# Second MoE product of eight token blocks in seven half-size products instead of eight, with operand sums on GpSimd and new orders

## The chip, the cores and the metric

The kernel runs on one core of a Trainium2 chip. TensorE (PE; its weight loads are shown as PEld), VectorE (DVE), ScalarE (ACT) and GpSimd (POOL) compute, and SyncE (SP) issues nearly all DMAs. The metric is the time of one execution on the device in microseconds, as the median of several runs.

## The reference, cut to what matters

Attention over 8 batches, 8 heads and 1152 positions of 64 numbers, with queries averaged in pairs; its output, 4608 tokens of 512 numbers, goes through a small MoE: the larger of two products, and a second product of that.

```python
q_pool = q.reshape(B, H, S // 2, 2, D).mean(axis=3)
scores = q_pool @ k.transpose(0, 1, 3, 2) / sqrt(D)
attn = softmax(scores) @ v                                   # exp, divided by its row sum
x = attn.transpose(0, 2, 1, 3).reshape(4608, 512)
g = np.maximum(x @ w1, x @ w2)                               # 4608 x 1024
out = g @ w_out                                              # 4608 x 512
```

All inputs and the output are float32.

## The kernel before, in words

**Recording.** The kernel is written as a list of operations, each with the keys that it reads and writes (`Plan.op`). `reorder` then puts each engine's operations in an order that is written out by hand as a text, one letter or digit for each operation (`pe_order`, `dve_order`, `act_order`, `pool_order`, `sp_order`), and `solve` sets the semaphore waits. Every engine works through its own list in order. A digit in `pe_order` is the PSUM bank on which a job does its next piece; `jobs_of` lists which jobs follow each other on a bank. S is a score group.

**Attention.** Heads are handled in 32 pairs. For each pair K, Q and V are loaded in float32 (three buffers each) and cast to bf16 on POOL: `cast_k` (L457), `cast_q` (the sum of two neighbours, L490), `cast_v` (L496). K is transposed by a DMA on the SP queue (L476). Q is transposed on VectorE by `qtrans_dve` (L546) in eight pieces of 32 partitions and 9 x 32 elements, since a transpose there works inside blocks of 32 x 32. The scores are made in 324 groups of 512 columns for both heads (L678): two matmuls run side by side, one on each half of the array's rows (a *duo*). ScalarE takes the exponential of each group (L685), out of three PSUM tiles, from group 21 on out of two. The averages over V (a, L589 with 128 rows, L601 for the last half tile) take nine matmuls of 65 columns a piece; a pair has two jobs, of five and four pieces. VectorE divides (L611, L615, L619), and the result is transposed to `xT`, mostly by DMA (L725), in part on TensorE (L737).

**MoE.** The larger of two products is rewritten: with wd = w1 - w2, g = relu(x wd) + x w2, so that out = relu(x wd) w_out + x (w2 w_out). wd is made on POOL (L770) and w21 = w2 w_out on TensorE (L802). The first product is done in 13 token blocks (H while scores last, as duos, L877; h afterwards, with all rows, L850); its rectified tiles go to `gT`, a ring of 1024 tokens. The second product (P, L910) takes 256 tokens at a time: 12 steps of contraction (4 of x with w21, 8 of gT with w_out), each with two token tiles of 128 on two banks, and each once for each half of the rows: 24 duos of 512 columns. The halves are swapped between the two *turns*, and the first matmul of the second turn waits for the first turn to end (`fence`). VectorE copies both banks out at once (L919) and SP stores them. The last six tiles are done one by one with all rows (p, L940), after the last score group.

Of the kernel before, what the change touches and what calls it, by code (L numbers as in the profile page):

```python
# [9 lines left out]
P = 128  # L10
# [9 lines left out]
class Plan:  # L20
# [26 lines left out]
    def lane(self, o):  # L47
# [3 lines left out]
        if o["eng"] == "POOL":  # L51
            return {"kb": "k", "wd": "d"}.get(key[:2], key[0])
# [5 lines left out]
        return {"qt": "T", "w2": "W", "wo": "W", "gd": "G"}.get(key[:2], "Q")  # L58
# [234 lines left out]
def bass_funnel_attn__then__act_maxout2_kernel(  # L293
# [23 lines left out]
    RING = 1024  # L317
    assert D == 64 and S == NT * P and QU == NT and C == H * D and E == 512
# [13 lines left out]
    with outer:  # L332
# [23 lines left out]
        xT = sbuf([P, NC_, NTOK], BF16, "xT")  # L356
# [6 lines left out]
        w2b = xT[:, :, 512:1536]  # L363
        w2T = xT[:, :, 1536:2560].rearrange("p c (f x) -> p c f x", x=P)
        w2f = xT[:, :, 2560:4608].bitcast(FP32)
# [3 lines left out]
        osb = [osb2[:, s, :] for s in range(4)]  # L369

# [132 lines left out]
        def dve(fn, r, w):  # L503
            op("DVE", fn, r=r, w=w)
# [35 lines left out]
        def qtrans_dve(i, n):  # L540
            s, z = i % 2, i % 3
            h, pb, db = n // 4, n // 2 % 2, n % 2
            src, dst = 64 * h + 32 * pb, 64 * h + 32 * db
            view = qpT[z][:, :].rearrange("p (u x) -> p u x", x=HP)
            last = [f"qpT{z}"] + (["qpT0.0"] if i == 3 else []) if n == 7 else []
            op("DVE", lambda e: e.transpose(  # L546
                view[dst:dst + 32, :, 32 * pb:32 * pb + 32],
                qpf[s][src:src + 32, :, 32 * db:32 * db + 32]),
                r=[f"qp{s}.0", f"qp{s}.1"], w=[f"qt{z}.{n}"] + last, after=[f"qpT{z}"] + (["qpT0.0"] if i == 3 else []))
# [114 lines left out]
        def skeys(g):  # L664
            return [key for i, t, lo, *_ in pieces(g) for key in (
                f"kT{i % 3}.{t}", "qpT0.0" if i == 0 and lo < QA else f"qpT{i % 3}")] + [
                f"qt{i % 3}.{n}" for i in pairs_of(g) if i >= Q_PE for n in range(8)]
# [62 lines left out]
        def xtrans_pe(i):  # L730
# [9 lines left out]
            def evac(m):  # L740
                mb = fb[m][:, :].bitcast(BF16)
                op("DVE", lambda e: e.tensor_copy(xT[:, ct, b * SQ:b * SQ + SQ], mb[:, 0:SQ]),  # L742
# [4 lines left out]
        def xkeys(ct, n0, n1):  # L747
            return [f"xT.{ct}.{j}" for j in range(n0 // HP, n1 // HP)]
# [40 lines left out]
        ocount = [0]  # L789
# [24 lines left out]
        def store(lo, s, c0=0, c1=E, engs=("SP", "SP")):  # L814
# [436 lines left out]
```

## Time and profile before

| what | us |
|---|---|
| median of 3 runs (lowest, highest) | 362.35 (362.02, 362.59) |
| span of the profiled execution | 361.7 |
| first and last exponential begin | 6.4, 329.8 |
| last score matmuls begin | 329.2 |
| last matmuls end | 358.6 |
| K, Q, V loads, from issue to landing (median) | 6.4, 6.0, 6.3 |

The granted clock of TensorE is 0.999 over the span. Score groups run from about 6 to 330 us; all other matmuls stand between them in `pe_order`, and the last block's share of the MoE follows them. In the prediction a row of a timeline has the start, the duration, the engine, the line, the operation, the tiles (written<-read), the shape and the count of merged instructions; a row of a group has the total of busy time, the mean of one in ns, and the idle time before them with what ended it. A row of the waits has the waiting engine and line, whom it waited for, the total, and how many times.

### The profile page before, as it was taken

To read this page: it belongs to the slowest core of one execution; us is meant where nothing else is said; L and a number is where in the kernel's file an instruction comes from. 1 tells how busy PE (TensorE), PEld (TensorE's weight loads), DVE (VectorE), ACT (ScalarE), POOL (GpSimd) and SP (SyncE) were. 2 spreads that over 40 slices of the span, in tenths; PEclk is the share of its full clock that TensorE was granted. 3 is DMA by queue.
4 is the path that set the end of the run, shared out by engine and by line. 5 is a ranking of instruction groups with operands and counts; after the bars stand their busy time and mean duration, and the time that the engine had idled before them with its cause. 6 is when DMAs were issued, how large, how long until landed. Compare 5 with 4: busy or idle time off the path is not lost.

```text
span 361.7 us, 13398 instructions
## 1 busy us (share of the span) xinstructions
PE 355.0 (98%) x5973; PEld 222.1 (61%) x5973; DVE 243.1 (67%) x528; ACT 313.3 (87%) x355; POOL 124.5 (34%) x111
## 2 busy tenths in 40 slices
PE   8899999999999999999999999999999999999996
PEld 6666655566564666657575666666666565656753
DVE  3676787877589777866876687595977747625411
ACT  5999989989999999998999999989999988994221
POOL 1248967333055324452242426261234440010000
PEclk9999999999999999999999999999999999999999
DMA  7999999999959998997999999998999560805215
GB/s 239 408 394 398 402 286 296 244 286 344 246 123 242 284 302 235 251 256 179 285 309 184 269 277 284 305 251 202 243 215 269 169 153 15 198 16 87 52 30 147
DMA packets 77789, 84.76 MB, mean 234 GB/s; under 512 B 50080, under 2 KB 50848, under 8 KB 77728
## 3 DMA queue, kind: packets, MB, share of 16 engines
q1 hardware_dynamic: 77168, 83.09, 87.6%
q8 instruction: 47, 0.77, 0.9%
q10 hardware_dynamic: 560, 0.79, 0.6%
q14 instruction: 14, 0.11, 0.1%
HBM read 62.91 MB, written 9.44 MB: 200 GB/s over the span
## 4 chain that ended last, share of the span: by engine, by line
PE 93%; ACT 5%; issue 0%; DVE 0%; DVEq 0%
PE sps L678 20%; PE sps L589 13%; PE sps L910 12%; PE fb L910 10%; PE sps L877 9%; PE fb L589 7%; PE fb L877 7%; ACT et L685 5%; PE sps L940 3%; PE sps L601 2%; PE fb L802 2%; PE fb L940 1%; PE sps L850 1%; PE fb L601 1%; PE fb L850 1%; PE fb L411 1%
## 5 line engine op out<-in xcount | busy, mean ns | idle before, releaser
L685 ACT ACTIVATE et<-sps 128x1024 bf16<-128x1024 f32 (+1 forms) x336 | 305.2, 1009 | 20.5 <-PE sps L678 19.3
L678 PE MATMUL sps<-qpT,kT 64*128 64x256 bf16 (+7 forms) x1162 | 119.8, 284 | 1.7 <-DVE qpT L536 0.7
L546 DVE STREAM_TRANSPOSE qpT<-qp 32x288 bf16<-32x288 bf16 x216 | 101.4, 469 | 4.5
L678 PEld LDWEIGHTS sps<-qpT,kT 64*128 64x128 bf16 x1162 | 47.3, 94 | 51.1 <-ACT et L685 19.9
L490 POOL TENSOR_TENSOR qp<-qraw 128x576 bf16<-128x576 f32 x30 | 42.2, 1406 | 83.1 <-DVE qpT L546 58.6
L496 POOL TENSOR_SCALAR vE<-vraw 128x1152 bf16<-128x1152 f32 x32 | 36.8, 1152 | 62.8 <-DMA vraw<-in_v_dram 48.1
L589 PE MATMUL sps<-vE,et 128*128 128x65 bf16 x1440 | 51.2, 193 | 0.6 <-issue 0.4
L589 PEld LDWEIGHTS sps<-vE,et 128*128 128x128 bf16 x1440 | 46.0, 97 | 6.9 <-issue 5.4
L457 POOL TENSOR_SCALAR kbf<-kraw 128x1152 bf16<-128x1152 f32 x31 | 35.6, 1151 | 42.2 <-DMA kraw<-in_k_dram 29.6
L877 PE MATMUL sps<-xT,wd 64*128 64x512 bf16 (+3 forms) x368 | 42.8, 326 | 0.1
L910 PE MATMUL sps<-wo,stage 64*128 64x512 bf16 x256 | 37.5, 377 | 0.0
L877 PE MATMUL fb<-xT,wd 64*128 64x512 bf16 (+3 forms) x272 | 33.0, 334 | 0.1
L887 DVE TENSOR_SCALAR stage<-sps 128x1024 bf16<-128x1024 f32 (+3 forms) x23 | 22.3, 969 | 15.4 <-PE sps L877 15.2
L910 PE MATMUL fb<-wo,stage 64*128 64x512 bf16 x224 | 32.5, 377 | 0.0
L589 PE MATMUL fb<-vE,et 128*128 128x65 bf16 x864 | 30.5, 193 | 0.0
L589 PEld LDWEIGHTS fb<-vE,et 128*128 128x128 bf16 x864 | 27.5, 97 | 4.2 <-issue 3.2
L887 DVE TENSOR_SCALAR stage<-fb 128x1024 bf16<-128x1024 f32 (+3 forms) x17 | 17.0, 999 | 10.4 <-PE fb L877 10.1
L877 PEld LDWEIGHTS sps<-xT,wd 64*128 64x128 bf16 x368 | 15.6, 94 | 12.0 <-DVE xT L742 0.8
L611 DVE RECIPROCAL rcs<-sps 128x5 f32<-128x5 f32 (+1 forms) x40 | 7.3, 183 | 19.4 <-PE sps L589 18.7
L919 DVE COPY stage<-sps 128x1024 f32<-128x1024 f32 x8 | 9.8, 1224 | 13.8 <-PE sps L910 13.8
L910 PE MATMUL sps<-w,xT 64*128 64x512 bf16 x128 | 18.6, 377 | 0.0
L910 PE MATMUL fb<-w,xT 64*128 64x512 bf16 x112 | 18.1, 377 | 0.0
(94 smaller groups left out, 286.3 us busy)
## 6 DMA issues: line engine op xcount, KB each, us to landing
vraw<-in_v_dram SPq DMA_DIRECT2D x32, 576.0 KB, 6.3
kraw<-in_k_dram SPq DMA_DIRECT2D x31, 576.0 KB, 6.4
qraw<-in_q_dram SPq DMA_DIRECT2D x31, 576.0 KB, 6.0
out_dram<-stage SPq DMA_DIRECT2D x21, 256.0 KB, 5.4
out_dram<-stage SPq DMA_DIRECT2D x23, 128.0 KB, 3.0
xT<-in_moe_w_dram SPq DMA_DIRECT2D x4, 512.0 KB, 10.7
stage<-in_moe_w_out_dram SPq DMA_DIRECT2D x4, 512.0 KB, 13.7
stage<-in_moe_w_dram SPq DMA_DIRECT2D x4, 512.0 KB, 13.4
```

Source lines behind the costliest of these rows:

```text
L457: op("POOL", lambda g: g.tensor_scalar(kbf[s][:, :, :, :].rearrange("p t h d -> p h t d"), kraw[r][:, :, :, :], 1.0, 1.0, ALU.mult, ALU.mu ...
L490: op("POOL", lambda g: g.tensor_tensor(qpf[s][:, :, :], qraw[r][:, :, 0, :], qraw[r][:, :, 1, :], ALU.add), r=[f"qraw{r}"], w=[f"qp{s}.0", ...
L496: op("POOL", lambda g: g.tensor_scalar(vE[r][:, :, :, 0:D].rearrange("p t h d -> p h t d"), vraw[r][:, :, :, :], 1.0, 1.0, ALU.mult, ALU.m ...
L546: op("DVE", lambda e: e.transpose(view[dst:dst + 32, :, 32 * pb:32 * pb + 32], qpf[s][src:src + 32, :, 32 * db:32 * db + 32]), r=[f"qp{s}. ...
L589: last = e.matmul(fb[m][:, sb * 66:sb * 66 + 65], et[:, a:a + P], vE[vs][:, t, half, 0:65], start=(t == 0), stop=(t == NT - 1))
L601: last = e.matmul(fb[m][rows(half), NCH * 66:NCH * 66 + 65], et[:, a:a + NB], vE[vs][:, t, half, 0:65], start=(t == 0), stop=(t == NT - 1))
L678: last = e.matmul(sps[r][:, h, col:col + hi - lo], kT[i % 3][rows(h), t, :], qpT[i % 3][rows(h), lo:hi], start=True, stop=True)
L685: op("ACT", lambda e: e.activation(et2[:, :, c:c + z - a], sps[r][:, :, a - g * W:z - g * W], EXP, scale=scale), r=[f"s{r}"], w=keys + ([f ...
L877: last = e.matmul(fb[m + k][:, 0:size], wd[z, ct, (f0 + k) * P:(f0 + k + 1) * P], xT[z, ct, n0:n1], start=(turn == 0 and ct == 0), stop=(t ...
L887: dve(lambda e: e.tensor_scalar_max(gT[:, f0:f0 + 2, g0:g0 + size], wide[m // 2][:, :, 0:size], 0.0), [f"f{m}", f"f{m + 1}"], w + [f"f{m}" ...
L910: last = e.matmul(fb[m + k][:, :], lhs, rhs, start=(turn == 0 and j == 0), stop=(turn == 1 and j == NC_ + NF - 1))
L940: return e.matmul(fb[m][:, 0:c1 - c0], lhs, rhs[:, c0:c1], start=(j == 0), stop=(j == NC_ + NF - 1))
```

## The change

Tokens 512 to 4607 are now handled in eight blocks of 512 (`p_block`), by the Winograd form of Strassen's scheme. The four token tiles are split into rows 0 (tiles 0 and 2) and 1 (tiles 1 and 3), the contraction into two halves of six steps, the output into two halves of 256 columns. Seven products of a quarter of the size give the block; each has 6 steps x 2 token tiles x 2 row halves = 24 matmuls of 256 columns, 12 duos. Four jobs hold them (two, two, two and one products); tokens 0 to 511 are still done by `p_pair` (named P0.5 and P256.5), and the tiles that were done one by one at the end now belong to the last two blocks.

The operands that are sums are made on POOL: `t_sums` once for the weights (4 sums in two parts), `s_sums` for each block (4 sums in two parts, of 512 elements from `xT` and of 1024 from `gT`; where a ring's end cuts a block, in two pieces). VectorE adds the products up while it empties the banks (`end1` to `end4`).

To make room `xT` becomes a ring of 2304 tokens, and the float32 copy of w2 moves to a tile `extra`, where the sums live later. The query transposes become one of the full 128 x 576 tile and four that put the off-diagonal 32 x 32 corners right. All four engines' order texts, `sp_order` and the jobs' banks are new.

```diff
+    XRING = NTOK // 2
+    KT = (NC_ + NF) // 2
...
-        xT = sbuf([P, NC_, NTOK], BF16, "xT")
+        xT = sbuf([P, NC_, XRING], BF16, "xT")
+        extra = sbuf([P, NC_ * XRING], BF16, "extra")
...
         def qtrans_dve(i, n):
...
-            op("DVE", lambda e: e.transpose(
-                view[dst:dst + 32, :, 32 * pb:32 * pb + 32],
-                qpf[s][src:src + 32, :, 32 * db:32 * db + 32]),
+            if n == 0:
+                dst, src = qpT[z][:, :], qpf[s].rearrange("p u d -> p (u d)")
+            else:
+                h, pb = (n - 1) // 2, (n - 1) % 2
+                db = 1 - pb
+                to, at = 64 * h + 32 * db, 64 * h + 32 * pb
+                dst = view[to:to + 32, :, 32 * pb:32 * pb + 32]
+                src = qpf[s][at:at + 32, :, 32 * db:32 * db + 32]
+            op("DVE", lambda e: e.transpose(dst, src),
...
+        def t_sums(n, at):
...
+            op("POOL", lambda g: g.tensor_tensor(t(n), one, two, ALU.subtract),
+               r=r, w=[f"tw{n}.{at}"], after=[f"w2f{c}" for c in range(NC_)], fence=True)
...
+        def s_sums(lo, n, at):
+            t0, t1 = ((0, 2), (2, KT))[at]
+            a11, a12, a21, a22 = ((0, 0), (0, 1), (1, 0), (1, 1))
+            one, two, alu, dst = ((a21, a22, ALU.add, 0), (0, a11, ALU.subtract, 1),
+                                  (a11, a21, ALU.subtract, 2), (a12, 1, ALU.subtract, 1))[n]
...
+                op("POOL", lambda g, js=js, view=view: g.tensor_tensor(
+                    sx[dst][:, t0:t1, js, :], view(one, v1), view(two, v2), alu),
+                    r=r1 + r2, w=[f"sx{dst}.{at}"], after=[f"w2f{NC_ - 1}", f"wof{NC_ - 1}"], fence=True)
+
+        def p_block(lo):
...
+                def pair(e, m):
+                    for t in ts:
+                        for k in range(2):
+                            z = rows(turn ^ k)
+                            lhs, rhs = left(a, k, t)[0], right(b, t)[0]
+                            last = e.matmul(
+                                fb[m + k][:, x * HE:x * HE + HE], lhs[z, :], rhs[z, :],
+                                start=opening and t == 0, stop=closing and t == KT - 1)
+                    return last
...
+            def end1(m):
+                dve(lambda e: e.tensor_copy(part[:, :, 0, :], bank(m, X0)), [f"f{m}", f"f{m + 1}"], ["p1"])
+                add(m, part[:, :, 1, :], part[:, :, 0, :], bank(m, X1), ["p1"], ["u2"], True)
...
+            def end4(m):
+                if final:
+                    for j in range(2):
+                        add(m, osb[2 * j][:, HE:E], part[:, j, 1, :], bank(m, X0)[:, j, :], ["u2"], [f"osb{2 * j}"],
+                            j == 1)
+                        store(lo + 2 * j * P, 2 * j, HE, E, ("SP", "ACT"))
+                    return
...
+            return [Job(stage_units(ps), end) for ps, end in (
+                (((X0, A11, B11), (X1, 1, 1)), end1),
+                (((X0, A12, B21), (X1, 2, 2)), end2),
+                (((X0, 0, 0), (X1, A22, 3)), end3),
+                (((X0, 1, B22),), end4))]
...
-            "4": "p3840.0",
+            "4": "h10.3 h10.7 P3584.0 h11.0 h11.5 P4096.2",
...
-            "qvvqkkqvv")
+            "rsqksvqsskvrrqkvqkvssssrkqssvqskssrvqkvssqkvrsqkssqksrvvsvsrssssrssrssrsssrsssss")
```

Three places show what the new orders move. The first is TensorE between score groups 225 and 233, where the averages of pair 21 stand (L589 and L601, now L604 and L616; scores L678, now L693; second product L910, now L995). A row is the line, the operation, written<-read, the size that is written, and the count. Before:

```order
L910 MATMUL fb<-wo,stage 128x512 x6
L678 MATMUL sps<-qpT,kT 128x512 x2
L910 MATMUL fb<-wo,stage 128x512 x4
L678 MATMUL sps<-qpT,kT 128x64 x2
L678 MATMUL sps<-qpT,kT 128x448 x2
L601 MATMUL sps<-vE,et 64x65 x18
L589 MATMUL sps<-vE,et 128x65 x36
L678 MATMUL sps<-qpT,kT 128x128 x2
L678 MATMUL sps<-qpT,kT 128x384 x2
L678 MATMUL sps<-qpT,kT 128x192 x2
L678 MATMUL sps<-qpT,kT 128x320 x2
L589 MATMUL sps<-vE,et 128x65 x36
```

Now:

```order
L616 MATMUL sps<-vE,et 64x65 x18
L693 MATMUL sps<-qpT,kT 128x256 x4
L604 MATMUL sps<-vE,et 128x65 x36
L693 MATMUL sps<-qpT,kT 128x320 x2
L693 MATMUL sps<-qpT,kT 128x192 x2
L693 MATMUL sps<-qpT,kT 128x384 x2
L693 MATMUL sps<-qpT,kT 128x128 x2
L604 MATMUL sps<-vE,et 128x65 x36
L693 MATMUL sps<-qpT,kT 128x448 x2
L693 MATMUL sps<-qpT,kT 128x64 x2
L995 MATMUL fb<-w,xT 128x256 x4
L995 MATMUL fb<-wo,stage 128x256 x8
```

The two stretches of averages of pair 21 have become three, with score groups between.

The second place is the end of POOL's list. Before, the casts of the last pairs end it:

```order
L490 TENSOR_TENSOR qp<-qraw 128x576
L457 TENSOR_SCALAR kbf<-kraw 128x2x9x64 x2
L490 TENSOR_TENSOR qp<-qraw 128x576
L496 TENSOR_SCALAR vE<-vraw 128x2x9x64 x2
L1192 TENSOR_LOAD flag
```

Now sums of operands (L963; 512 elements from xT, 1024 from gT, which lies in `stage`) end it:

```order
L963 TENSOR_TENSOR stage<-xT 128x512
L963 TENSOR_TENSOR extra<-xT,extra 128x512
L963 TENSOR_TENSOR extra<-stage,extra 128x1024
L963 TENSOR_TENSOR extra<-xT 128x512
L963 TENSOR_TENSOR stage<-stage 128x1024
L963 TENSOR_TENSOR extra<-stage 128x1024
L963 TENSOR_TENSOR extra<-extra,xT 128x512
L963 TENSOR_TENSOR extra<-extra,stage 128x1024
L963 TENSOR_TENSOR extra<-xT,extra 128x512
L963 TENSOR_TENSOR extra<-stage,extra 128x1024
L1382 TENSOR_LOAD flag
```

Behind the last cast of V there are now 22 sums, for the last three blocks; the rows shown are S2 (small) of the last block, S3 of the block before, and then S0, S2, S1 and S3 of the last.

The third place is the end of TensorE's list. Before, the last tile's full-row matmuls end it:

```order
L940 MATMUL sps<-wo,stage 128x512 x6
L940 MATMUL sps<-wo,stage 128x384
L940 MATMUL sps<-wo,stage 128x512 x3
L940 MATMUL sps<-wo,stage 128x384 x7
L940 MATMUL sps<-w,xT 128x128 x4
L940 MATMUL sps<-wo,stage 128x128 x8
```

Now the last block's products do, those with a sum as left operand reading `extra`:

```order
L995 MATMUL sps<-w,xT 128x256 x4
L995 MATMUL sps<-wo,stage 128x256 x8
L995 MATMUL sps<-extra 128x256 x16
L995 MATMUL fb<-wo,stage 128x256 x8
L995 MATMUL fb<-extra,stage 128x256 x12
L995 MATMUL sps<-extra 128x256 x8
L995 MATMUL sps<-extra,xT 128x256 x4
L995 MATMUL sps<-extra,stage 128x256 x8
L995 MATMUL sps<-w,extra 128x256 x4
L995 MATMUL sps<-wo,extra 128x256 x8
L995 MATMUL sps<-w,extra 128x256 x4
L995 MATMUL sps<-wo,extra 128x256 x8
```

The last 24 matmuls are the product of S3, the sum that POOL makes last; ahead of them stand the products of S0, S1 and S2 of the same block.

More of the change, by code (lines that the diff above doesn't have):

```diff
@@ L501, in unit, with dve @@
             return lambda m: op("PE", lambda e: go(e, m), r=r, w=[f"f{m}"])
-        def dve(fn, r, w):
-            op("DVE", fn, r=r, w=w)
+        def dve(fn, r, w, after=()):
+            op("DVE", fn, r=r, w=w, after=after)
         def qtrans(i):
@@ L747, in xkeys @@
         def xkeys(ct, n0, n1):
-            return [f"xT.{ct}.{j}" for j in range(n0 // HP, n1 // HP)]
+            return [f"xT.{ct}.{j % (XRING // HP)}" for j in range(n0 // HP, n1 // HP)]
         def w_load(part, c):
@@ L878, in pair @@
                                 fb[m + k][:, 0:size], wd[z, ct, (f0 + k) * P:(f0 + k + 1) * P],
-                                xT[z, ct, n0:n1], start=(turn == 0 and ct == 0),
+                                xT[z, ct, n0 % XRING:n0 % XRING + size], start=(turn == 0 and ct == 0),
                                 stop=(turn == 1 and ct == NC_ - 1))
@@ new lines, in tiles, with akeys, ablocks @@
+        def tiles(lo, row):
+            return [lo + (2 * j + row) * P for j in range(2)]
+        def akeys(lo, row, k, at):
+            ns = tiles(lo, row)
+            if at == 0:
+                return [key for n in ns for c in range(2) for key in xkeys(2 * k + c, n, n + P)]
+            return [f"gT.{n % RING // P}.{4 * k + f}" for n in ns for f in range(4)]
+        def ablocks(lo, row, k, at):
+            src, w, size = ((xT, 2, XRING), (gT, 4, RING))[at]
+            full = src[:, k * w:k * w + w, :]
+            a = lo % size
+            if a + 4 * P <= size:
+                return [(slice(0, 2), full[:, :, a:a + 4 * P].rearrange("p t (j r x) -> p t j r x", r=2, x=P)[
+                    :, :, :, row, :])]
+            return [(slice(j, j + 1), full[:, :, n % size:n % size + P].unsqueeze(2))
+                    for j, n in enumerate(tiles(lo, row))]
@@ L1071, in chores, with fed @@
                 if i >= Q_PE:
-                    later(f"q{i}", [f"cq{i}"], lambda i=i: [qtrans_dve(i, n) for n in range(8)], free)
+                    later(f"q{i}", [f"cq{i}"], lambda i=i: [qtrans_dve(i, n) for n in range(5)], free)
                 if f"x{i}" not in on_pe:
                     later(f"x{i}", [f"a{i}"] + over(i), lambda i=i: xtrans(i))
+            ready = [f"wc{n}.{ct}" for n, ct in W_CASTS] + [f"wd{ct}.{half}" for ct, half in W_DIFFS]
+            for n in range(4):
+                for at in range(2):
+                    later(f"t{n}.{at}", ready + ["W0", "W2"][:2 - 2 * at] + [f"t{m}.{at}" for m in range(n)],
+                          lambda n=n, at=at: t_sums(n, at))
+            units = sorted({int(name[1:-2]) for v in jobs_of.values() for name in v.split()
+                            if name[0] == "P" and name.endswith(".0")})
+            for lo, back in zip(units, [None] + units):
+                def fed(row, k, lo=lo):
+                    return [f"H{nb}.{f}" if f"H{nb}" in count else f"h{nb}.{f + g}"
+                            for nb, (n0, n1) in enumerate(hblocks)
+                            if any(n0 < n + P and n < n1 for n in tiles(lo, row))
+                            for f in range(4 * k, 4 * k + 4, 2) for g in ((0,) if f"H{nb}" in count else (0, 1))]
+                here = [f"x{i}" for i in range(lo // SQ * NHP, ((lo + 4 * P - 1) // SQ + 1) * NHP)]
+                for n, dst in enumerate((0, 1, 2, 1)):
+                    for at in range(2):
+                        own = (fed(1, 0) + fed(1, 1), fed(0, 0), fed(0, 0) + fed(1, 0), fed(0, 1))[n]
+                        need = ready + (own if at else here) + [f"s{lo}.{m}.{at}" for m in ((), (0,), (), (1,))[n]]
+                        if n == 3:
+                            need.append(f"P{lo}.0")
+                        elif back is not None:
+                            need.append(f"P{back}.{(2, 3, 1)[n]}")
+                        later(f"s{lo}.{n}.{at}", need, lambda lo=lo, n=n, at=at: s_sums(lo, n, at))
         def more_banks(groups):
@@ L1194, in bass_funnel_attn__then__act_maxout2_kernel @@
         engs = (("POOL", nc.gpsimd), ("SP", nc.sync), ("DVE", nc.vector), ("ACT", nc.scalar), ("PE", nc.tensor))
-        first = {"POOL": 33, "SP": 66, "DVE": 92, "ACT": 61, "PE": 208}
+        first = {"POOL": 33, "SP": 66, "DVE": 88, "ACT": 61, "PE": 208}
         early = {"SP": 7, "ACT": 12, "DVE": 3}
```

207 lines of the change are left out of this document (144 added, 63 removed), and 31 rows, old and new, of the table jobs_of.

## The prediction

> **What bounds the kernel now.** I read first the busy shares and the chain of work that ended last, on the page, then the busy time of each engine in two stretches: from the end of score group 72 to the end of the last exponential (75.8 to 330.8 us), and from there to the end.
>
> ```profile
> PE 355.0 (98%) x5973; PEld 222.1 (61%) x5973; DVE 243.1 (67%) x528; ACT 313.3 (87%) x355; POOL 124.5 (34%) x111
> PE 93%; ACT 5%; issue 0%; DVE 0%; DVEq 0%
> 75.80:330.80 255.00, 254.86 (x4415) 156.76 (x4412) 179.33 (x388) 238.15 (x261) 84.20 (x69) 1.00 0.92 226
> 330.80:361.70 30.90, 27.80 (x277) 18.23 (x275) 10.32 (x28) 6.04 (x17) 0.00 (x0) 0.99 0.31 74
> ```
>
> The columns of the last two rows are the stretch, its length, and then PE, PEld, DVE, ACT and POOL busy with counts, granted clock, DMA share and GB/s. TensorE is busy for 254.86 of 255 us, ScalarE for 238.15. Busy alone proves little, since matmuls overlap, so the waits decide:
>
> ```profile
> PEld sps L678 <- ACT et L685: 19.9, 74, 0.7
> ACT et L685 <- PE sps L678: 19.3, 40, 1.5
> ```
>
> (In total, times, the longest.) The weight load of a score group waits for ScalarE 74 times, 0.27 us each. A matmul of 512 columns streams for 0.38 us while the next weights are fetched, so such a wait is mostly covered. TensorE's matmul stream sets the time. ScalarE is close behind: 252 groups cost it 238.15 us, 0.945 each, against 255/252 = 1.012 on TensorE. I therefore add up what the change does to TensorE, and then ask whether ScalarE or a new wait ends later.
>
> **Streaming removed.** A duo is two half-row matmuls, one on each half of the array's rows, that run side by side.
>
> ```profile
> 329.44 1.46 PE L910 MATMUL fb<-wo,stage 64*128 64x512 bf16 x12
> 130.72 0.38 PE L910 MATMUL fb<-w,xT 64*128 64x512 bf16 x2
> 206.39 0.60 PE L877 MATMUL sps<-xT,wd 64*128 64x256 bf16 x8
> 202.67 0.27 PE L877 MATMUL sps<-xT,wd 64*128 64x256 bf16 x2
> ```
>
> Six duos of 512 columns take 1.46 us and one alone 0.38, so each further one takes (1.46-0.38)/5 = 0.216. At 256 columns it is (0.60-0.27)/3 = 0.110, and half of 0.216 is 0.108; I take 0.109. A block of 512 tokens had 48 duos of 512 columns (10.37 us). It now has seven products of 12 duos of 256 columns: 84 x 0.109 = 9.16. Eight blocks save 8 x 1.21 = **9.7 us**. Rows rounded to 0.01 us leave this between 7 and 11.
>
> Here a rule of the Trainium skill speaks against the change: in TensorE: Matmul & The Clock Gate, section Back-to-back issue gap, a real stream of weight loads and matmuls runs at about 81 ns per matmul at 128 columns and 131 ns at 512. An estimate between the two gives 98 ns at 256, and by that page a block would go from 96 x 0.131 to 168 x 0.098, 3.9 us longer. The row above, 8 matmuls in 0.60 us, does not agree.
>
> **Changes between full rows and half rows.** The averages (L589) use all rows, scores and duos half of them.
>
> ```profile
> 162.71 1.80 PE L589 MATMUL sps<-vE,et 128*128 128x65 bf16 x54
> 164.45 0.61 PE L678 MATMUL sps<-qpT,kT 64*128 64x512 bf16 x4
> ```
>
> The averages end at 164.51, the two score duos at 165.06: 0.55 us for 2 x 0.216, so 0.12 is lost at the change. I count the changes of row or column mode in the two orders: between score groups 72 and 324 there are 131 before and 155 now, because the averages are cut into more pieces between scores (pair 21 above), and behind the last score 2 and 10. That is 32 x 0.11 = **+3.5 us**. TensorEngine Tiling, section Key Properties, in the Trainium skill says that a change of tiling mode drains the engine; the row agrees, with 0.12 us. Were the changes free, the sum below would be 3.5 us lower.
>
> **Turns without cover.** A job swaps its row halves in the middle, and the second half waits for the first to finish.
>
> ```profile
> 133.66 0.40 PE L877 MATMUL sps<-xT,wd 64*128 64x128 bf16 x8
> 110.74 0.63 PE L877 MATMUL fb<-xT,wd 64*128 64x128 bf16 x8
> 111.02 0.17 PEld L877 LDWEIGHTS fb<-xT,wd 64*128 64x128 bf16 x6 [0.40 <-PE fb L877]
> ```
>
> Eight equal matmuls take 0.40 us without a turn among them and 0.63 with one. Where other work stands between the halves nothing is lost. By the order, turns with nothing between were 1 and are now 14 (10 ahead of the last score, 4 behind). 13 x 0.23 = **+3.0 us**; between 0 (if loads run ahead) and 3.9 (0.30 each).
>
> **Sums on GpSimd.** None of this shape is in the trace. The nearest rows:
>
> ```profile
> L490 POOL TENSOR_TENSOR qp<-qraw 128x576 bf16<-128x576 f32 x30 | 42.2, 1406 | 83.1 <-DVE qpT L546 58.6 <-DMA qraw<-in_q_dram 24.4
> L770 POOL TENSOR_TENSOR wd<-stage,xT 128x512 bf16<-128x512 f32 x8 | 10.0, 1272 | 0.1
> L496 POOL TENSOR_SCALAR vE<-vraw 128x1152 bf16<-128x1152 f32 x32 | 36.8, 1152 | 62.8 <-DMA vraw<-in_v_dram 48.1 <-PE sps L589 12.1 <-PE fb L589 2.6
> ```
>
> From 512 to 576 elements 134 ns are added, 2.1 ns each, so 512 elements cost 1.27 us and 1024 cost 0.20 + 1024 x 2.1 = 2.34. Two-input sums with bf16 operands lie between the one-input row (1 ns per element: 1024 in 1.02) and this; I take 1.27 and 2.34, the same operation. A block needs four of each, 14.4 us, the weights as much once, 131 us in all; some 40 us of it stand behind the last cast. In the long stretch POOL goes from 84 of 255 us to about 170 of 245. A waiting sum holds the casts queued behind it, for which the SP queue's K transposes, VectorE's query transposes and the averages wait. POOL's idle time of 171 us in that stretch is the cover; if it fails, every score group behind is late.
>
> Behind the last score the cover is thin. There the last block's sums form a chain: after the last rectified tile is evicted (0.42) come the large S0, then the small and the large S1, 5.95 us, with about 1 us of another sum ahead. Against that 7.3 us TensorE has 56 duos (6.1 us) and some 0.5 of changes and turns. Then S3, 3.6 us, is covered by 28 duos (3.1 us). That leaves 0.7 + 0.5; chains that start earlier take some off, and I take **+0.8 us**, between 0 (one-input rate) and 3.8 (no time lost on TensorE's side).
>
> **VectorE.** Each pair's eight transposes become five.
>
> ```profile
> L546 DVE STREAM_TRANSPOSE qpT<-qp 32x288 bf16<-32x288 bf16 x216 | 101.4, 469 | 4.5
> L919 DVE COPY stage<-sps 128x1024 f32<-128x1024 f32 x8 | 9.8, 1224 | 13.8 <-PE sps L910 13.8
> L967 DVE COPY stage<-sps 128x512 f32<-128x512 f32 x1 | 0.7, 692 | 1.8 <-PE sps L940 1.8
> ```
>
> 108 pieces go (-50.7 us) and 27 full ones come, at 0.47 to twice that (+13 to +25). Seven evictions of a block cost about 6 x 0.69 + 1.22 = 5.4 us against 2 x 1.22, +24 in all. VectorE at 179 of 255 us stays about where it is: **0**. A bank pair is held for two operations, 1.4 us instead of 1.2; the other pair's matmuls hide this, and each time they don't costs about 0.2. DMA: as many bytes are loaded and stored, and the SP queue's stores go out once per block instead of twice; 0.
>
> **ScalarE.** By column counts 15 us of matmuls leave the long stretch (13 of them second product), partly to the end, and 2.6 of changes and 2.1 of turns come in: TensorE falls from 255 to about 244.6, ScalarE's 238.15 stays. Three of fourteen stages fall under ScalarE's 17.0 us; **+0.3**, between 0 and 3.
>
> **The end.**
>
> ```profile
> 358.00 0.61 PE L940 MATMUL sps<-wo,stage 128*128 128x128 bf16 x8
> 358.75 0.29 DVE L954 COPY stage<-sps 128x128 f32<-128x128 f32 x1 [2.67 <-PE sps L940]
> L619 DVE TENSOR_TENSOR xnat<-sps,rcs 128x256 bf16<-128x256 f32 x40 | 16.6, 423 | 1.1
> ```
>
> The last eviction took 0.29 us; now two additions of 256 columns follow each other, 2 x 0.42. **+0.6 us**.
>
> **Sum.** -9.7 + 3.5 + 3.0 + 0.8 + 0 + 0.3 + 0.6 = -1.5 on the profiled span of 361.7, so 360.2. The median of the runs is 362.35, 0.65 above the span, which I keep: **360.8 us**.
>
> **The rivals.**
> *The losses are hidden.* Turns cost nothing, the chain at the end is covered, and the changes go at 0.08: -9.7 + 2.6 + 0.6 = -6.5, so 355.9. For it: most turns that had work beside them show no loss. Against: the 0.63 us row.
> *POOL ends last (slower).* If the 1024-element sum takes 3.2 us and the small one 1.7, the two chains of the last block overrun by 3.0 and 1.9, and that of the block before by about 1.5: 6.4 instead of 0.8, so 366.4. It decides from a large sum of about 2.75 us, where the loss eats the 1.5 us gained. For it: strided operands, which no row shows. Against: both two-input rows lie on one line.
> *ScalarE hides the gain.* Stages of 18 groups before:
>
> ```profile
> 220.30:237.80 17.50, 16.91 (x20) 1.00 1.08 308
> 274.50:293.50 19.00, 16.97 (x20) 1.00 0.76 190
> ```
>
> Columns: stretch, length, ScalarE busy. Even the shortest is 0.6 us above ScalarE's own work. If all fourteen stages end at about 17.6, the stretch takes 246.4 instead of 244.9, and the whole 362.3: no change.
> *Weight loads bind at 256 columns.* A load takes 94 ns (below); were loads not overlapped, 84 duos would take 84 x 0.188 = 15.8 us a block, 43 us more in all: 405. The skill's issue-gap figures above lie on this side. The 0.60 us row speaks against it.
>
> ```profile
> L910 PEld LDWEIGHTS sps<-wo,stage 64*128 64x128 bf16 x256 | 12.1, 94 | 9.4
> ```
>
> That the products aren't cut is no rival: the order has 1344 matmuls of 256 columns for what 768 of 512 did.
>
> **How the numbers follow.** Forecast 45%, spread over some 358.5 to 363; hidden losses 20%; ScalarE 16%; POOL 17%; weight loads 2%. About 0.2%, 0.72 us, is what a measurement of this kernel can tell. Faster (below 361.6): 0.35 of the forecast, 0.19 and 0.03, so 0.57. Same: 0.09 and 0.11, 0.20. Slower: 0.23. The range runs from the hidden losses, 355.5, to 365.0, short of POOL's full price, which leaves out under 2 in 10.
>
> **What would show it.** Right: duos of 256 columns at 0.11 us; the last exponential near 322 and not 331; nearly 40 us behind it instead of 31; TensorE waiting for POOL only near the end. Wrong: large sums not at 2.3 us; score groups waiting for casts; TensorE idle for ScalarE through the long stretch; a last exponential near 315, which would mean that turns and changes cost less than I put down.

## The result, and the profile after

The changed kernel takes 377.19 us (375.66 to 378.85, 4 runs); the kernel before took 362.47 in the same series (362.02 to 362.63). The ratio is 1.040, 95% interval 1.037 to 1.044: slower. The profiled execution, the slowest of the four, has a span of 377.6 us, 17.4 above the 360.2 of the forecast's sum. One execution of a later run (e11, 433.48 us) had a granted clock of 0.75, and its ratio leaves it out.

From the page of the changed kernel, the busy shares, the granted clock in 40 slices and the chain of work that ended last; then two stretches, from score group 72 to the end of the last exponential and from there to the end (columns as in the prediction):

```profile
PE 357.8 (95%) x6609; PEld 250.1 (66%) x6609; DVE 237.0 (63%) x488; ACT 312.6 (83%) x351; POOL 241.0 (64%) x187
PEclk9999999999999699999998999999999999999999
PE 68%; POOL 12%; issue 9%; ACT 5%; DVE 3%; DMA 2%; SPq 0%; POOLq 0%; DVEq 0%
78.10:337.97 259.87, 251.33 (x4773) 175.49 (x4766) 164.93 (x338) 238.85 (x262) 165.43 (x124) 0.98 0.86 210
337.97:377.60 39.63, 33.70 (x567) 27.91 (x563) 20.43 (x47) 3.92 (x13) 24.70 (x15) 0.98 0.34 85
```

TensorE's share of the chain fell from 93% to 68%, and GpSimd, which was not in it, has 12%. The part behind the last exponential is 39.6 us, as forecast (nearly 40). The loss is ahead of it: the last exponential ends at 338.0 instead of near 322. In that stretch TensorE is idle for 8.5 us, against 0.14 before, and the clock dips twice. GpSimd's load there, 165 us, is what was forecast (170). These rows of the waits tell for whom TensorE is idle, for whom GpSimd is, and what holds the K transposes on SyncE's queue (total, times, longest); L457 and L476 are the kernel before:

```profile
PE sps L995 <- POOL extra L963: 3.9, 4, 2.7
PE fb L995 <- POOL extra L963: 2.8, 1, 2.8
PE fb L616 <- DVE w L824: 1.5, 1, 1.5
POOL kbf L467 <- DMA kT<-kbf: 40.7, 15, 5.1
POOL kbf L457 <- DMA kT<-kbf: 12.5, 5, 4.8
SPq L486 <- PE sps L693: 49.5, 22, 7.6
SPq L476 <- PE sps L678: 23.8, 12, 5.9
```

The products (L995) wait for sums (L963), and GpSimd itself is idle for 40.7 us, in front of casts of K that may not overwrite one of the two `kbf` buffers before the DMA transpose has read it. The transposes don't take longer than before (5.3 us from issue to landing in the median, 6.0 before); 22 of the 27 first wait on SyncE's queue until TensorE's scores have freed a `kT` tile, so that TensorE itself is part of what GpSimd waits for. Here is how the one becomes the other, on GpSimd's timeline, and then TensorE's row that waits:

```profile
102.33 1.15 POOL L467 TENSOR_SCALAR kbf<-kraw 128x1152 bf16<-128x1152 f32 x1 [3.60 <-DMA kT<-kbf]
103.44 1.41 POOL L500 TENSOR_TENSOR qp<-qraw 128x576 bf16<-128x576 f32 x1
104.82 1.15 POOL L506 TENSOR_SCALAR vE<-vraw 128x1152 bf16<-128x1152 f32 x1
110.47 1.15 POOL L467 TENSOR_SCALAR kbf<-kraw 128x1152 bf16<-128x1152 f32 x1 [4.50 <-DMA kT<-kbf]
111.59 2.13 POOL L963 TENSOR_TENSOR stage<-stage 128x1024 bf16<-128x1024 bf16 x1
113.67 1.40 POOL L500 TENSOR_TENSOR qp<-qraw 128x576 bf16<-128x576 f32 x1
117.67 1.15 POOL L467 TENSOR_SCALAR kbf<-kraw 128x1152 bf16<-128x1152 f32 x1 [2.59 <-DMA kT<-kbf]
118.78 1.16 POOL L506 TENSOR_SCALAR vE<-vraw 128x1152 bf16<-128x1152 f32 x1
119.90 2.12 POOL L963 TENSOR_TENSOR extra<-stage 128x1024 bf16<-128x1024 bf16 x1
122.10 2.12 POOL L963 TENSOR_TENSOR extra<-extra,stage 128x1024 bf16<-128x1024 bf16 x1
```

```profile
124.28 1.04 PE L995 MATMUL sps<-extra 64*128 64x256 bf16 x8 [2.67 <-POOL extra L963]
```

Three casts stand idle for 10.7 us in all, and the sum that ends at 124.2 stands behind them in the same queue. Its own 2.12 us are not what is late.

The idle of TensorE costs twice. Stretches in which the clock's records say 0.50, and four equal matmuls in one of them and just before it:

```profile
123.36:130.19 6.83, 5.85 (x54) 3.78 (x56) 1.15 (x2) 2.37 (x3) 5.31 (x5) 0.50 1.54 213
205.28:208.69 3.41, 3.41 (x36) 2.45 (x34) 0.00 (x0) 1.58 (x2) 2.23 (x2) 0.50 1.03 219
201.02 0.38 PE L995 MATMUL fb<-w,xT 64*128 64x256 bf16 x4
206.18 0.64 PE L995 MATMUL fb<-w,xT 64*128 64x256 bf16 x4
```

After each of the two idles of about 3 us the clock stands at half for 6.83 and for 3.41 us; half of the busy time in them, 2.9 and 1.7 us, is lost. So far the loss adds up to 6.7 (sums) + 4.6 (clock) + 1.5 (VectorE) = 12.8 of 17.4 us, by one profile. The theory of the queue was that the first two are one cause and its consequence; the rivals were that the sums are too much work for GpSimd, and that the products themselves cost more than was forecast.

### The profile page after: what moved, and what is told of

Read it like the earlier page. It is cut to its first block, busy times and chain, and to the rows that moved or that the text cites. A ratio compares the mean times of both kernels' runs of the same rounds, so it can differ in the third digit from the quotient of the medians.

```text
span 377.6 us, 14733 instructions
## 1 busy us (share of the span) xinstructions
PE 357.8 (95%) x6609; PEld 250.1 (66%) x6609; DVE 237.0 (63%) x488; ACT 312.6 (83%) x351; POOL 241.0 (64%) x187
## 4 chain that ended last, share of the span: by engine, by line
PE 68%; POOL 12%; issue 9%; ACT 5%; DVE 3%; DMA 2%; SPq 0%; POOLq 0%; DVEq 0%
PE sps L693 15%; PE sps L995 11%; PE sps L604 8%; PE fb L604 7%; PE fb L995 6%; PE sps L893 6%; POOL extra L963 5%; ACT et L700 5%; PE fb L893 4%; POOL qp L500 2%; POOL vE L506 2%; PE sps L866 2%; PE fb L817 2%; PE fb L1081 1%; POOL kbf L467 1%
## 5 line engine op out<-in xcount | busy, mean ns | idle before, releaser
L693 PE MATMUL sps<-qpT,kT 64*128 64x256 bf16 (+7 forms) x1162 | 122.9, 286 | 1.8 <-DVE qpT L546 0.7
L562 DVE STREAM_TRANSPOSE qpT<-qp 32x288 bf16<-32x288 bf16 (+1 forms) x135 | 71.6, 530 | 13.9 <-PE sps L693 10.0
L693 PEld LDWEIGHTS sps<-qpT,kT 64*128 64x128 bf16 x1162 | 48.1, 95 | 34.0 <-ACT et L700 9.8
L467 POOL TENSOR_SCALAR kbf<-kraw 128x1152 bf16<-128x1152 f32 x31 | 35.7, 1153 | 46.9 <-DMA kT<-kbf 40.7
L604 PEld LDWEIGHTS sps<-vE,et 128*128 128x128 bf16 x1188 | 38.2, 97 | 8.3 <-issue 6.5
L604 PE MATMUL sps<-vE,et 128*128 128x65 bf16 x1188 | 43.0, 193 | 0.7 <-issue 0.5
L893 PE MATMUL sps<-xT,wd 64*128 64x512 bf16 (+3 forms) x352 | 40.2, 330 | 0.8 <-DMA xT<-xnat 0.6
L604 PE MATMUL fb<-vE,et 128*128 128x65 bf16 x1116 | 40.0, 193 | 0.0
L604 PEld LDWEIGHTS fb<-vE,et 128*128 128x128 bf16 x1116 | 35.7, 97 | 6.5 <-issue 5.7
L893 PE MATMUL fb<-xT,wd 64*128 64x512 bf16 (+3 forms) x288 | 33.3, 335 | 0.2
L1022 DVE TENSOR_TENSOR stage<-stage,sps 128x512 f32<-128x512 f32 (+2 forms) x30 | 23.1, 774 | 9.8 <-PE sps L995 8.9
L995 PE MATMUL sps<-extra 64*128 64x256 bf16 x288 | 21.9, 280 | 3.6 <-POOL extra L963 3.6
L893 PEld LDWEIGHTS sps<-xT,wd 64*128 64x128 bf16 x352 | 15.3, 96 | 12.6 <-PE sps L893 2.1
L963 POOL TENSOR_TENSOR stage<-stage 128x1024 bf16<-128x1024 bf16 x8 | 17.0, 2125 | 6.3 <-DVE stage L903 6.2
L963 POOL TENSOR_TENSOR extra<-xT 128x512 bf16<-128x512 bf16 (+1 forms) x9 | 9.4, 1047 | 16.1 <-DVE bad L1350 8.9
L995 PEld LDWEIGHTS sps<-extra 64*128 64x128 bf16 x288 | 13.7, 97 | 7.8 <-POOL extra L963 4.4
```

The costliest lines, as they stand in the source:

```text
L467: op("POOL", lambda g: g.tensor_scalar(kbf[s][:, :, :, :].rearrange("p t h d -> p h t d"), kraw[r][:, :, :, :], 1.0, 1.0, ALU.mult, ALU.mu ...
L562: op("DVE", lambda e: e.transpose(dst, src), r=[f"qp{s}.0", f"qp{s}.1"], w=[f"qt{z}.{n}"] + last, after=[f"qpT{z}"] + (["qpT0.0"] if i == ...
L604: last = e.matmul(fb[m][:, sb * 66:sb * 66 + 65], et[:, a:a + P], vE[vs][:, t, half, 0:65], start=(t == 0), stop=(t == NT - 1))
L693: last = e.matmul(sps[r][:, h, col:col + hi - lo], kT[i % 3][rows(h), t, :], qpT[i % 3][rows(h), lo:hi], start=True, stop=True)
L893: last = e.matmul(fb[m + k][:, 0:size], wd[z, ct, (f0 + k) * P:(f0 + k + 1) * P], xT[z, ct, n0 % XRING:n0 % XRING + size], start=(turn == ...
L963: op("POOL", lambda g, js=js, view=view: g.tensor_tensor(sx[dst][:, t0:t1, js, :], view(one, v1), view(two, v2), alu), r=r1 + r2, w=[f"sx{ ...
```

## The experiments

| run | us, median (lowest, highest) | ratio to before, 95% interval |
|---|---|---|
| e1 third K buffer | 370.73 (366.96, 372.10) | 1.019 (1.013, 1.025) |
| e2 six K casts later | 372.87 (371.85, 373.76) | 1.028 (1.025, 1.031) |
| e3 no sums of activations | 369.71 (368.39, 371.12) | 1.020 (1.017, 1.024) |
| e4 before, new query transposes | 363.55 (362.55, 364.38) | 1.002 (1.000, 1.004) |
| e5 e1 and VectorE's order | 371.00 (369.75, 371.14) | 1.022 (1.018, 1.026) |
| e6 e5, code shifted by 164 | 373.50 (372.67, 373.92) | 1.028 (1.024, 1.033) |
| e7 before, products in halves | 367.13 (366.22, 368.43) | 1.011 (1.007, 1.016) |
| e8 e7 with few V loads | 364.30 (363.72, 364.96) | 1.003 (1.001, 1.005) |
| e9 e5 with few V loads | 364.26 (363.70, 366.19) | 1.004 (1.002, 1.006) |
| e10 before with few V loads | 362.19 (361.73, 363.62) | 0.998 (0.996, 0.999) |
| e11 changed, few V loads | 364.99 (364.71, 433.48) | 1.006 (1.004, 1.008) |

**e1, a third K buffer.** Its room is the unused half of the two `qp` tiles.

```diff
-kbf = [sbuf([P, NT, 2, D], BF16, f"kbf{s}") for s in range(2)]
+kbf = [sbuf([P, NT, 2, D], BF16, f"kbf{s}") for s in range(3)]
...
-later(f"ck{i}", [f"lk{i}", f"ck{i - 1}"] + old("k", i, 2), lambda i=i: cast_k(i))
+later(f"ck{i}", [f"lk{i}", f"ck{i - 1}"] + old("k", i, 3), lambda i=i: cast_k(i))
```

> The changed kernel with a third buffer for the bf16 K tiles, so that GpSimd's cast of K for a pair no longer waits for the DMA transpose of the pair two before it. Queue theory (the sums are late because they stand in GpSimd's queue behind casts that wait for that DMA; TensorE then idles 3.0 + 3.0 + 0.7 + 0.9 us for sums and runs some 5 us longer at a lower granted clock behind the two long idles): the waits of TensorE for sums before the last exponential shrink to under 1 us in all, no dip of the clock in that stretch, about 364.5 us (363 to 367). Size theory (the sums of 1.16 and 2.13 us are simply too much for GpSimd between two products): the waits move but stay, 373 to 378 us. Product theory (the short matmuls, mode changes and weight loads cost more than was forecast, sums are no matter): no change, 376 to 378 us.

370.73, 6.5 us less than the changed kernel. The idle of GpSimd for DMA transposes of K, 40.7 us, is gone from the waits, TensorE's matmuls wait for sums for 0.3 us instead of 6.7, and the two dips of the clock are gone. So the size theory falls: the same sums on the same engine are in time. But 364.5 was expected, and some 6 us were left. The profile shows where: an idle of 2.14 us for VectorE at 57.9 us (1.95 in the bracket of the profile's row), with 3.41 us at half clock behind it, and idles of 0.5 to 1.4 us at 112, 144, 186 and 253 us, for nothing that the profile shows ("issue"), some of them in the middle of a job.

**e2, only the order on GpSimd.** Two of its places, positions 56 to 68 and 100 to 108 of the order (k a cast of K, s and r sums, q and v the other casts):

```diff
-kqvkrqkvssqvk   rsqksvqss
+kqvrqkvsskqvk   rsqskvqss
```

> The changed kernel, still with two K buffers, in which six casts of K stand one to three places later in GpSimd's queue, behind the sums that they held up; nothing else is different. Queue theory: both 3 us waits of TensorE for sums go, and the clock stays up there; about 366 us (364 to 369), somewhat more than with the third buffer since the other casts still wait. Size theory: the same work is on the same engine, so 374 to 378 us. Product theory: 376 to 378 us.

372.87: between the theories. Both 3 us idles are gone, and the clock stays up at both places. A longer one has come at the next place where sums stand behind a cast; GpSimd's timeline, and TensorE's row:

```profile
154.62 1.15 POOL L467 TENSOR_SCALAR kbf<-kraw 128x1152 bf16<-128x1152 f32 x1 [6.17 <-DMA kT<-kbf]
155.73 1.40 POOL L500 TENSOR_TENSOR qp<-qraw 128x576 bf16<-128x576 f32 x1
157.10 2.13 POOL L963 TENSOR_TENSOR stage<-stage 128x1024 bf16<-128x1024 bf16 x1
159.19 2.11 POOL L963 TENSOR_TENSOR extra<-stage 128x1024 bf16<-128x1024 bf16 x1
161.28 1.15 POOL L506 TENSOR_SCALAR vE<-vraw 128x1152 bf16<-128x1152 f32 x1
162.39 2.11 POOL L963 TENSOR_TENSOR extra<-extra,stage 128x1024 bf16<-128x1024 bf16 x1
```

```profile
164.56 0.82 PE L995 MATMUL sps<-extra 64*128 64x256 bf16 x6 [4.85 <-POOL extra L963]
```

In the changed kernel the cast at this place waited 5.08 us too, but TensorE, late by the losses ahead of it, waited only 0.16 us for the sum. Behind this idle the clock stood at half for 6.83 us. The mechanism is the expected one; that mending two places would be enough was wrong.

**e3, no sums of activations.** The products read a plain tile where a sum belongs.

```diff
-later(f"s{lo}.{n}.{at}", need, lambda lo=lo, n=n, at=at: s_sums(lo, n, at))
+later(f"s{lo}.{n}.{at}", need, lambda: None)
```

> The changed kernel without the three operand sums of activations (the products take a plain tile where a sum belongs, so the output is another); TensorE, VectorE and ScalarE do the same instructions as in the changed kernel. This gives the price of TensorE's side alone. Queue theory and size theory: no wait for sums is left, the time comes to what the forecast's sum gives without its GpSimd term and with the waits that VectorE's order makes near 58 and 72 us, 360 to 363 us. Product theory: the loss stays, over 370 us.

369.71: neither number. Without any sum of activations 7.5 us are gained, about what e1 gains with all of them (6.5); so the sums account for about half of the loss. The same two stretches, and two of TensorE's rows:

```profile
77.77:328.79 251.02, 246.54 (x4773) 173.24 (x4766) 165.18 (x338) 237.80 (x262) 86.59 (x71) 1.00 0.92 217
328.79:368.10 39.31, 33.43 (x567) 28.04 (x563) 20.51 (x47) 3.92 (x13) 0.00 (x0) 0.98 0.34 86
182.87 0.23 PE L604 MATMUL sps<-vE,et 128*128 128x65 bf16 x2 [1.14 <-issue]
249.76 0.40 PE L693 MATMUL sps<-qpT,kT 64*128 64x384 bf16 x4 [1.17 <-issue]
```

TensorE is still idle for 4.5 us in the long stretch. The second row stands inside one score group, whose first matmuls ran 1.3 us earlier. A group is one operation and waits for its data and its buffer ahead of its first matmul, so neither can be missing there. That spoke for something that neither the forecast nor the three theories had.

**A new theory: TensorE's code.** The trace has packets of 16,384 bytes on a queue of kind "instruction", 47 before and 52 after the change. At 64 bytes an instruction (two queue entries per matmul, a weight load and the matmul itself, with a few semaphore entries, give 13,289 for 52 packets in e3) a packet holds 256. I numbered TensorE's entries and set each unexplained idle beside the last packet that landed:

| run | idle begins, us | length | entry behind it, mod 256 | behind the packet's landing |
|---|---|---|---|---|
| e3 | 141.0 | 0.66 | 168 | 1.51 |
| e3 | 181.7 | 1.32 | 169 | 1.53 |
| e3 | 248.6 | 1.33 | 168 | 1.42 |
| e1 | 144.1 | 1.41 | 169 | 1.34 |
| e1 | 185.6 | 1.02 | 168 | 1.48 |
| e6 | 67.1 | 3.80 | 6 | 1.33 |
| e6 | 255.0 | 1.13 | 6 | 1.36 |
| e7 | 135.7 | 1.07 | 170 | 1.31 |
| e7 | 220.1 | 1.23 | 170 | 1.37 |

Within a kernel each stands at the same place of a block of 256, and each resumes 1.3 to 1.5 us after a packet has landed. (These lengths are 0.16 to 0.20 us more than the brackets of the rows, 1.32 against 1.14 at 181.7 us; idles for nothing are given in this way in the text on the runs.) The packet of the next block starts after the running block has begun, up to 5 us later, and takes 1 us. So one block is fetched ahead, and TensorE waits if it runs through 256 entries in less than this delay, the transfer and the 1.3 to 1.5 us together. The shortest such run ahead of 330 us took 5.6 us before the change and 4.9 after it, since two matmuls of 256 columns take four entries in 0.11 us and two of 512 took four in 0.22.

The Trainium skill, Runtime: NRT & Kernel Launch, section Instruction fetch mechanics, says that the sequencer refills in blocks of 16 KiB, 256 instructions, by a DMA queue of its own, and that the cost of crossing a block is mostly hidden. The block size agrees; that it is hidden does not, with 0.7 to 1.4 us, once 3.8, at the crossings above.

**e5 and e6, VectorE's place, then the code shifted.** On VectorE the cast of w21 (the 0 below) that TensorE waits for at 58 us stood behind two query transposes (T), and these behind GpSimd's query sum.

```diff
-TTTTT6TT0TTT6
+TTTTT60TTTTT6
```

> The changed kernel with the third K buffer of the first experiment and, besides, the cast of w21 on VectorE put ahead of two query transposes that wait for GpSimd's query sum (one place in VectorE's order). Queue theory, now for VectorE too: the idle of TensorE near 58 us (2.14 us in the run with the third buffer, with 3.41 us at half clock behind it) goes, and the clock is full from there to the end; 2 to 4 us off that run's 370.7, so 366.5 to 369. What is left over the forecast are TensorE's idles in the middle of a group with nothing to wait for, 0.4 to 1.4 us each. Product theory (the loss is in the products themselves): no gain beyond 0.5 us.

e6 changes one number besides, the place in a block of 256 at which TensorE's code goes on behind its branch:

```diff
-nc.tensor.addr_align(2 * P, offset=0, max_nops=0)
+nc.tensor.addr_align(2 * P, offset=164, max_nops=0)
```

> The kernel of the run before with one number changed: TensorE's code after its branch starts 164 instructions further on in a block of 256, so the ends of the 16 KB blocks in which its code is loaded fall on other instructions; no engine does anything else. Code theory (the idles with nothing to wait for are waits for the next 16 KB of TensorE's code, asked for when the block before it begins, and late where 256 instructions go by in 5 us while the DMA queues are full): the idles stand at an instruction number of 4 or 5 in a block of 256 instead of 168 or 169, each 1.3 to 1.6 us behind the landing of a 16 KB packet of the instruction queue; the sum of them changes by 1 us or so. Any other theory (data, buffers, another engine): the idles stay with the instructions at which they stood.

e5: the idle at 58 us and the dip behind it are gone, and the profiled span is 368.4 against e1's 370.9. But the medians, 371.00 and 370.73, don't differ: e1's runs spread over 5 us, and its profiled one had a long idle there. So the place is worth 2.5 us between the two profiles, and nothing that the medians show; 2 to 4 was a miss. e6: the idles for nothing stand at 5 or 6 of 256, four of them over 0.3 us, and none at 168 to 170 any more. That settles where they come from: no instruction, operand or order differs from e5. The sum of these idles rose from 2.7 to 5.6 us, where a change of 1 us or so was expected; the longest stands at the first end of a block behind the branch (a block that the shift has cut to 92 entries):

```profile
70.69 1.00 PE L602 MATMUL fb<-vE,et 128*128 128x65 bf16 x15 [3.60 <-issue]
255.99 0.72 PE L993 MATMUL sps<-extra 64*128 64x256 bf16 x10 [0.96 <-issue]
```

The first of them again drew 6.83 us of half clock behind it.

**e7, short matmuls alone.** In the kernel before:

```diff
-                        last = e.matmul(fb[m + k][:, :], lhs, rhs, start=(turn == 0 and j == 0),
-                                        stop=(turn == 1 and j == NC_ + NF - 1))
+                        both.append((fb[m + k], lhs, rhs))
+                    for x in range(2):
+                        at = slice(x * (E // 2), x * (E // 2) + E // 2)
+                        for to, lhs, rhs in both:
+                            last = e.matmul(to[:, at], lhs, rhs[:, at], start=(turn == 0 and j == 0 and x == 0),
+                                            stop=(turn == 1 and j == NC_ + NF - 1 and x == 1))
```

> The kernel before with each 512-column matmul of its paired second products split into two of 256 columns: the same columns, the same order, no sums, no further mode changes, and 1440 instructions of TensorE more (the change has 1272 more). Code theory: the windows of 256 instructions in the products get shorter (5.1 us at the least instead of 5.6), so two to five idles of 0.4 to 1.4 us appear that the kernel before does not have, 364.5 to 367 us. Product theory (a 256-column matmul costs more than half of a 512-column one): 0.01 us on each of 1440 more matmuls and loads at the least, over 375 us. If neither is so: 362 to 363.3 us.

367.13: 4.5 us more for the same columns, no sum and no new order. Five idles of 0.4 to 1.2 us have come, 3.5 us in all, each at 169 or 170 of 256; two of them:

```profile
136.55 0.40 PE L877 MATMUL sps<-xT,wd 64*128 64x128 bf16 x8 [0.90 <-issue]
221.15 0.28 PE L915 MATMUL fb<-wo,stage 64*128 64x256 bf16 x2 [1.06 <-issue]
```

The product theory's 375 is excluded. So most of the cost of the halves lies where the code runs out; the 1 us that is left of the 4.5 is not assigned.

**e4, the query transposes alone.** The kernel before with the change's `qtrans_dve`, its order without three of every eight transposes.

> The kernel before with the query transposes alone changed (one full and four corner pieces for the eight small ones, the order of everything else kept). All theories: VectorE is busy about 30 us less, and since no step of the stretch waits for it for long, the time is that of before within 1 us (361.5 to 363.5). If the transposes carry a part of the loss, it is over 365.

363.55, ratio 1.002: at the edge of what can be told from no change, 0.05 us above the expected range, and VectorE is busy for 213.0 instead of 243.1 us.

**e8 to e11, fewer data on the DMA queues.** What holds up the transposes of K and the packets of code? In four kernels 29 of the 32 V loads are left out:

```diff
-later(f"lv{i}", old("cv", i, 3), lambda i=i: load_v(i))
+later(f"lv{i}", old("cv", i, 3), lambda i=i: load_v(i) if i < 3 else None)
```

> The kernel before with the halved product matmuls of the run before, but V loaded for the first three pairs alone (29 of 32 loads of 576 KB left out, the stale V is used, so the output is another). TensorE's instructions and their order stay as they are. Code theory in the form that the next 16 KB of code wait behind data in the DMA queues: with a quarter of the data gone, the median delay from the end of a block to the start of its packet falls from some 2 us to under 1.3, the five idles of 0.4 to 1.2 us at 168 to 170 of 256 shrink to under 1 us in all, and the time falls to 362.5 to 364.5. If the code's own latency is what is too long, whatever the data do: the idles stay, 366 to 368 us.

> The same cut of V loads in the kernel with the third K buffer and VectorE's changed place (output again another). Code theory with data in its way: the three idles of 0.8 to 1.1 us at 169 or 170 of 256 go, and so do idles for late DMA transposes; 364 to 367 us, against 371.0. Latency theory: 369 to 371 us.

> The kernel before with the same cut of V loads, as the control of the two runs before (output another). It has no idle of TensorE over 0.3 us in the stretch that could go, so all theories have 361.5 to 363; if it falls to 358 or less, the cut of data itself is worth what the other two runs gained, and they say nothing of the code.

> The changed kernel as it is, with the same cut of V loads (output another). Queue theory: the cast of K still stands ahead of the sums, but the DMA transposes that it waits for land sooner; TensorE's waits for sums shrink from 7 us to 2 to 5, a clock dip may go; 367 to 373 us. If the sums were late because of their own duration, the waits stay and the time is over 374. If the code alone were the loss, it is 362 to 365.

The control, e10, is 0.24% faster than before. e8 gives back most of e7's loss (367.13 to 364.30); the median delay from the beginning of a block to the start of the next one's packet falls from 2.8 to 1.4 us (under 1.3 was expected), and two idles over 0.3 us are left of five, 1.2 us in all (under 1 was expected). e9 falls from 371.00 to 364.26; its delay from 2.7 to 0.9, and no idle over 0.3 us is left in the long stretch. So the latency theory falls: code is late because data are in its way. e11 is the surprise: the changed kernel itself, untouched but for the loads, falls from 377.19 to 364.99, below the 367 to 373 expected of the queue and inside the 362 to 365 written down for the code alone. The trace decides between the two. The row that answers to the 40.7 us above:

```profile
POOL kbf L467 <- DMA kT<-kbf: 10.1, 6, 4.6
```

TensorE's matmuls wait once for a sum, 0.3 us behind the last exponential, no dip is left ahead of it, and the code is late once by more than 0.3 us (0.93 us at 65.2). So 11 of the 13.9 us between the two profiles are waits for sums and half clock, as the queue theory says; it had left 2 to 5 us of these waits standing, and so it missed. The K transposes take 4.2 us from issue to landing instead of 5.3, and the delay of the code's packets falls from 1.7 to 0.9 (medians). That the sums, like the code, are late through the data on the queues is likely. But without the V loads SyncE also has 29 of its 234 DMAs less to issue, and no run parts that from the data; GpSimd's own waits for V stay (3.5 and 3.6 us).

## Why the prediction was wrong

The predicted 360.8 (355.5 to 365.0) was for a kernel in which almost nothing waits. e9 is nearly that kernel, with a quarter of the loads left out: all sums, all products, and its stretches are

```profile
76.35:323.40 247.05, 245.99 (x4773) 173.06 (x4767) 164.88 (x338) 237.57 (x262) 164.03 (x124) 1.00 0.71 162
323.40:362.90 39.50, 33.70 (x567) 27.96 (x563) 20.21 (x47) 3.91 (x13) 24.68 (x15) 0.97 0.34 86
```

with a span of 362.9 against the forecast's 360.2 and a last exponential that ends at 323.4 against 322. The terms one by one:

- **The step that failed** is "POOL's idle time of 171 us in that stretch is the cover". It counted the idle time and not what stands in it. In the kernel before, 161 us of it are waits: 88 for DMAs, 59 for VectorE's query transposes, 15 for TensorE. GpSimd takes its queue in order, so a sum that stands behind a waiting cast can't use that time. The text had the blocking the other way round ("A waiting sum holds the casts queued behind it"). In the kernel before, the 12.5 us for K transposes cost TensorE nothing (0.14 us of idle in the stretch), and in e4 GpSimd waits 29.4 us for them and TensorE 0.5 us for GpSimd: no sum stands behind those casts. Price in the changed kernel: 6.7 us of waits, and 4.6 of half clock, for which the sum had no term.
- **Streaming, -9.7.** Right in its rate: eight matmuls of 256 columns again take 0.60 us at full clock. But a second step failed here: the loading of code was put at nothing, and short matmuls use up code twice as fast. e7 prices that at 3.5 us of idles, 4.5 at the most, for 1440 additional instructions. In the profile of the changed kernel only two such idles stand, 0.56 and 0.74 us; that its long waits gave the packets time is likely, and not shown.
- **Turns, +3.0.** Borne out in part: the weight loads' waits for TensorE's own matmuls (sps and fb, L893 and L995, against L877 and L910 before) rose from 11 with 3.4 us to 21 with 6.8. That is ten more where the order gave thirteen, and 11 before where it gave one; at the 0.23 us that the forecast took for each, ten cost 2.3 us:

```profile
PEld sps L893 <- PE sps L893: 2.1, 7, 0.5
PEld fb L893 <- PE fb L893: 1.6, 5, 0.3
PEld sps L995 <- PE sps L995: 2.1, 6, 0.5
PEld fb L995 <- PE fb L995: 1.0, 3, 0.3
...
PEld fb L877 <- PE fb L877: 1.6, 5, 0.4
PEld sps L877 <- PE sps L877: 0.8, 3, 0.3
PEld sps L910 <- PE sps L910: 0.7, 2, 0.3
PEld fb L910 <- PE fb L910: 0.3, 1, 0.3
```

- **Sums, 2.34 and 1.27 us.** 2.13 and 1.16 (the rows of the timeline above and the group below), so the rival that needed 2.75 is out. The end lost 0.3 us to them and not 0.8: 39.6 us with them, 39.3 without (e3), and one wait of 0.33 us.

```profile
L963 POOL TENSOR_TENSOR stage<-stage x8: 2121/2125/2130, 111.6 to 358.1; 128x1024 bf16<-128x1024 bf16 x8
L963 POOL TENSOR_TENSOR extra<-xT x9: 669/1153/1157, 96.3 to 357.0; 128x512 bf16<-128x512 bf16 x7, 128x256 bf16<-128x256 bf16 x2
```

- **VectorE, 0.** Right for its load (164.9 us in the stretch; e4 for the transposes), wrong for its order: 1.5 us at 58 us, again a queue's head that waits for GpSimd.
- **The end, +0.6, and nearly 40 us behind the last exponential.** The whole came out, 39.6 us, but partly by luck. From the end of the last matmul to the end of the span it was 3.1 us before (358.6 to 361.7) and is 5.2 now (372.4 to 377.6, by the row below): 2.1 more and not 0.6. The last addition ends 0.8 us later behind the matmuls than the last copy did, and the rest passes until the last stores have landed. The forecast's own terms put the last exponential at 75.8 + 244.9 = 320.7; its "near 322" doesn't follow from them.

```profile
371.77 0.60 PE L995 MATMUL sps<-wo,extra 64*128 64x256 bf16 x8
```

- **Mode changes, +3.5, and ScalarE, +0.3.** Not priced by themselves. With only 1.06 us of idle left, e9's long stretch is 247.05 us and not 244.9. Whether mode changes or ScalarE (the rival in which the stretch takes 246.4) take these 2 us is open.

Of the 17.4 us above the forecast's span, then, 6.7 are waits for sums, 4.6 half clock, 1.5 VectorE's order, 1.0 code and 0.6 a late transpose of xT at 266 us (idles by the brackets of the rows). The last 3.0 are about what e9 keeps without them: 2.7, of which 2.2 lie in the long stretch and 0.5 ahead of it.

None of the variants beats the kernel before. Even with a quarter of the loads left out, e9 and e11 stay 0.4 to 0.6% above it, and 2.1 and 2.8 us above e10, the kernel before with the same loads. In e9 the long stretch is 8.0 us shorter than before and the part behind it 8.6 longer, so of the 9.7 us of streaming nothing is left over, even where nearly nothing waits.

## What to carry to other kernels

Idle time on an in-order engine is cover only for work that stands ahead of what the engine is waiting for: before new work goes there, list what each idle of it waits for and what would stand behind. Halving the columns of matmuls doubles the rate at which code is used; where the DMA queues are full (a share of 0.86 to 0.92 in the long stretches here, 0.71 in e9), look for idles with no releaser at equal places of 256 instructions. And an idle of a few us on TensorE is paid again in half clock, so the first late transfer costs more than its lateness.

## What was not expected of the hardware

- The granted clock fell to 0.50 after idles of 1.95 (e1), 2.67, 2.81 (changed kernel), 3.60 (e6) and 4.85 us (e2), by the brackets of the rows, for 3.41, 6.83, 3.41, 6.83 and 6.83 us, one or two times 3.41; after idles of 1.52 (changed kernel), 1.58 (e3) and 1.69 us (e2) it did not fall. The Trainium skill, TensorE: Matmul & The Clock Gate, section What's actually happening, gives a free-running window of 3413 ns, with which the lengths agree. The section HAM oscillation of the same page of the Trainium skill asks for no idle above some 3.4 us; here 1.95 us were enough.
- A 16 KB packet of code started up to 5 us after the block before its own had begun, and TensorE went on only 1.3 to 1.5 us after it had landed.
- 29 fewer V loads were worth 0.9 us (0.24%) to the kernel before and 12.2 us to the changed one.
